# Batches 1 to 7 of an attention and MLP kernel: values read where they lie, key scales by sums, global queries in pairs, and a planner's constants set anew

## The chip, the cores and the metric

The kernel runs on one core of a Trainium2 chip. It is one launch; the metric is the device time of that launch in microseconds (us). The engines that the text speaks of are TensorE (PE; its weight loads are listed as PEld), VectorE (DVE), ScalarE (ACT), GpSimd (POOL) and SyncE (SP), whose queue issues all transfers of this kernel.

## The reference

Attention with a window of 32 and 32 global tokens, over 8 batches and 8 heads, then an MLP with the mish function. Cut to what matters:

```python
k_all, v_all = [k_g, k_l], [v_g, v_l]          # 32 global tokens, 512 local ones, head size 64
out_g = sm(scale * q_g @ k_all.T) @ v_all      # global queries see all 544 keys
s_ll = where(|i - j| <= 32, scale * q_l @ k_l.T, -1e9)
out_l = sm([scale * q_l @ k_g.T, s_ll]) @ [v_g, v_l]
x = [out_g, out_l] as (8 * 544, 512)
h = x @ w_in                                   # 512 x 2048, 64-bit floats
out = (h * tanh(softplus(h))) @ w_out          # 2048 x 512, 64-bit floats
```

## The kernel before

**Attention.** The 8 heads go in pairs (`hp` 0 to 3), so there are 32 pairs (b, hp). Of each pair the 512 local queries are 4 tiles `t` of 128, which gives 128 units (b, hp, t). A tile's scores `s` cover a window of 192 or 224 keys, the global 32 among them (`WIN`). `row_max` masks them and takes the row's maximum on DVE, `expo` is the exponential on ACT, `p_hi` and `p_lo` split the probabilities into two fp16 numbers, `p_turn` transposes them by a DMA (batch 0 does it on PE, `p_pe`), and `pv` multiplies with the values into `U`. A tile's window is taken as two chunks of up to 128 keys. Their values lie in two tiles of their own, `va` and `vc`, which seven DMAs per pair (`v_move`, 416 KB) fill from the split values `vf`. `x_norm` divides, and `x` is transposed into `xx`, from which the MLP reads.

**Global queries.** `g_scores`, `g_max`, `g_exp`, `g_norm` and `g_turn` run once per pair, on 64 rows (2 heads of 32 queries). The stationary operand of `g_scores` is 128 columns wide from batch 2 on, of which the first 64 are used.

**Precision.** fp16 numbers come as a high and a low half, and a product takes three matmuls (hi hi, hi lo, lo hi). The scores of batches 0 and 1 are fp32 matmuls instead (`plain_s`); from batch 2 on `b_norm` takes scales for queries and keys from the largest absolute value of the batch, over 8 loads of 272 KB.

**MLP.** 16 blocks of 256 tokens (two per batch) and one of all global tokens, each in 8 steps: 24 matmuls into `h` (`m1_mm`), mish on ACT into `e` (`mish`), a split into `GG` on DVE (`g_hi`, `g_lo`), 12 matmuls into `o` (`m2_mm`). `h` and `e` have two buffers each, `GG` holds 16 steps. The last three blocks use 7 products in place of 8 (`product`).

**Weights.** They arrive as 64-bit floats in 32 loads of 512 KB (16 for each matrix). Each is turned into fp32 by one ACT instruction and two on DVE (`w_bits`, `w_sum`), enters a norm on PE (`w_stat`), and when the 16 of a matrix are through, `w_norm` sets the scale (one `wd` instruction on DVE begins it) and `w_split` makes the fp16 halves. `h` needs the splits of the first matrix, `o` those of the second.

**Order.** The code does not run in the order in which it is written. `slot(u)` hands tasks with costs to a planner (`Plan`), which works through them by list scheduling and emits each engine's instructions in the order that its plan gives. The first loads stand in `ORDER`, a weight load waits until the planned DMA backlog is under `BULK` ns, and constants such as `CONV1` and `RATE1` give the weights' tasks their places. The planner may also put idle matmuls (`w_s<-consts`) in front of a waiting PE task in the first part. Each engine works its list strictly in order, and the SP queue does too: a DMA that waits for its source holds back all behind it.

Of the kernel before, what the change touches and what calls it, by code (L numbers as in the profile page):

```python
# [1490 lines left out]
```

## Time and profile before

| | |
|---|---|
| median of 3 runs | 925.22 us (923.16 to 926.66) |
| profiled execution: its own time | 922.33 us |
| its span, first to last instruction | 920.5 us |
| PE busy | 894.3 us (97%) |
| DVE, ACT busy | 726.4 us (79%), 612.0 us (66%) |
| mean granted clock of TensorE | 0.988 |
| transfers on the SP queue's ring | 130.65 MB |

Busy PE time is the union of modelled matmul spans. 1.8 us of the profiled execution's time lie outside the span. The profiled execution is 0.8 us under the fastest of the three timed runs and 2.9 us under their median.

### The profile page before, as it was taken

To read this page: it belongs to the slowest core of one execution; us is meant where nothing else is said; L and a number is where in the kernel's file an instruction comes from. 1 tells how busy PE (TensorE), PEld (TensorE's weight loads), DVE (VectorE), ACT (ScalarE), POOL (GpSimd) and SP (SyncE) were. 2 spreads that over 40 slices of the span, in tenths; PEclk is the share of its full clock that TensorE was granted. 3 is DMA by queue.
4 is the path that set the end of the run, shared out by engine and by line. 5 is a ranking of instruction groups with operands and counts; after the bars stand their busy time and mean duration, and the time that the engine had idled before them with its cause. 6 is when DMAs were issued, how large, how long until landed. Compare 5 with 4: busy or idle time off the path is not lost.

```text
span 920.5 us, 21758 instructions
## 1 busy us (share of the span) xinstructions
PE 894.3 (97%) x8444; PEld 649.5 (71%) x8444; DVE 726.4 (79%) x1940; ACT 612.0 (66%) x1309; POOL 18.0 (2%) x30
## 2 busy tenths in 40 slices
PE   4989999999999999999999999999999999999998
PEld 2767866666767766766766766776776776788887
DVE  6999988868878779787987788877876757798761
ACT  5899786877777768776787768776776667322110
POOL 3000000000000000000000000000000000000000
PEclk9799999999999999999999999999999999999999
DMA  9987358987665878667767867777855554100000
GB/s 331 316 260 254 97 138 161 193 185 185 151 147 123 185 162 179 125 154 172 165 128 153 169 158 162 134 184 165 185 114 124 95 88 77 31 13 2 23 13 35
DMA packets 221399, 132.03 MB, mean 143 GB/s; under 512 B 174320, under 2 KB 186736, under 8 KB 221296
## 3 DMA queue, kind: packets, MB, share of 16 engines
q1 hardware_dynamic: 221296, 130.65, 61.6%
q8 instruction: 66, 1.08, 0.5%
q14 instruction: 37, 0.30, 0.1%
HBM read 66.76 MB, written 8.91 MB: 82 GB/s over the span
## 4 chain that ended last, share of the span: by engine, by line
PE 76%; DVE 8%; DMA 7%; ACT 6%; issue 2%; SPq 1%; POOL 0%; ACTq 0%; DVEq 0%
PE h L985 31%; PE o L1050 26%; PE o L1146 5%; PE U L843 4%; PE s L747 3%; PE g L877 2%; DMA pt<-ph 2%; ACT P L771 1%; DMA mx<-in_mxs 1%; PE gu L942 1%; DVE GG L1038 1%; DVE GG L361 1%; SPq L348 1%; DVE P L762 1%; ACT e L1018 1%
## 5 line engine op out<-in xcount | busy, mean ns | idle before, releaser
L985 PE MATMUL h<-xx,W 128*128 128x256 f16 x3072 | 361.6, 273 | 0.3 <-DMA xx<-xs 0.2
L985 PEld LDWEIGHTS <-W 128*128 128x128 f16 x3264 | 311.4, 98 | 43.0 <-issue 4.3
L1050 PE MATMUL o<-W,GG 128*128 128x512 f16 x1344 | 314.5, 379 | 0.9 <-ACT ob L359 0.9
L1050 PEld LDWEIGHTS <-GG 128*128 128x128 f16 x1344 | 128.7, 98 | 128.5 <-issue 2.4
L1018 ACT ACTIVATE e<-h,c 128x512 f32<-128x512 f32 x136 | 92.7, 687 | 125.1 <-PE h L985 108.2
L771 ACT ACTIVATE P<-P,nm 128x192 f32<-128x192 f32 (+1 forms) x256 | 117.6, 461 | 57.8 <-DVE nm L762 56.4
L1038 DVE SCALAR_TENSOR_TENSOR GG<-e,c,GG 128x512 f16<-128x512 f32 (+1 forms) x136 | 111.3, 819 | 3.6
L361 DVE TENSOR_SCALAR GG<-e,c 128x512 f16<-128x512 f32 (+1 forms) x130 | 78.4, 604 | 39.5 <-ACT e L1018 35.1
L762 DVE CUSTOM_DVE_ANT_0 P<-s,consts 128x192 f32<-128x192 f32 (+1 forms) x256 | 87.5, 364 | 4.4 <-PE s L747 4.4
L826 DVE SCALAR_TENSOR_TENSOR ph<-P,ph 128x448 f16<-128x448 f32 (+1 forms) x112 | 62.8, 587 | 23.2 <-ACT ph L359 22.1
L843 PEld LDWEIGHTS <-pt 96*128 96x128 f16 (+1 forms) x1536 | 60.0, 98 | 27.6 <-issue 5.4
L1018 ACT ACT_TABLE_LOAD x55 | 70.6, 1283 | 3.6 <-PE h L985 2.6
L843 PE MATMUL U<-va,pt 128*128 128x64 f16 (+1 forms) x768 | 56.0, 193 | 2.6 <-DMA pt<-ph 2.1
L359 ACT ACTIVATE ph<-P 128x384 f16<-128x384 f32 (+1 forms) x111 | 55.2, 535 | 0.8 <-DMA pt<-ph 0.7
L843 PE MATMUL U<-vc,pt 96*128 96x64 f16 x768 | 55.4, 193 | 0.0
L1146 PEld LDWEIGHTS <-GG 128*128 128x128 f16 x504 | 49.2, 98 | 6.8 <-DVE GG L1038 1.1
L771 ACT ACTIVATION_READ_ACCUMULATOR P<-P,nm 128x1 f32 x256 | 48.1, 188 | 0.0
L359 ACT ACTIVATE ob<-o,c 128x512 f32<-128x512 f32 (+1 forms) x40 | 24.6, 615 | 32.2 <-PE o L1146 26.7
L771 ACT ACT_TABLE_LOAD x34 | 43.6, 1283 | 0.6
L616 DVE TENSOR_REDUCE mx<-mx 128x1 f32<-128x544 f32 x48 | 34.3, 714 | 10.2 <-DMA mx<-in_mxs 10.2
L1146 PE MATMUL o<-W,GG 128*128 128x256 f16 x360 | 41.6, 273 | 0.5 <-DVE GG L1038 0.5
L359 ACT ACTIVATE xg<-gu,sv 64x32 f32<-64x32 f32 x64 | 20.0, 313 | 24.0 <-PE gu L942 23.5
(159 smaller groups left out, 1029.5 us busy)
## 6 DMA issues: line engine op xcount, KB each, us to landing
mx<-in_mxs SPq DMA_DIRECT2D x48, 272.0 KB, 3.1
out<-ob SPq DMA_DIRECT2D x34, 256.0 KB, 2.9
vl<-in_vm SPq DMA_DIRECT2D x32, 256.0 KB, 4.3
W<-in_w SPq DMA_DIRECT2D x15, 512.0 KB, 6.9
...
GG<-in_w SPq DMA_DIRECT2D x11, 512.0 KB, 5.8
```

The costliest lines, as they stand in the source:

```text
L359: A.activation(out=dst, in_=src, func=AF.Copy, scale=c)
L361: V.tensor_scalar(dst, src, c, None, ALU.mult)
L616: pl.add(DVE, dve(544), lambda i=i, k=k: V.tensor_reduce(out=X[mx][:, i:i + 1], in_=X[k][:, :544], axis=AX.X, op=ALU.max, apply_absolute_v ...
L762: pl.add(DVE, 69 + 1.04 * w, lambda: V.tensor_tensor_reduce(out=X[P][:, h, :w], in0=X[s][:, c], in1=mask[:, m0:m0 + w], scale=-SCALE, scal ...
L771: pl.add(ACT, 94 + 0.832 * w + 186, lambda: A.activation(out=X[P][:, h, :w], in_=X[P][:, h, :w], func=AF.Exp, bias=X[nm], scale=-1.0, accu ...
L826: pl.add(DVE, dve(n), lambda: V.scalar_tensor_tensor(p_part(X[ph], t, 1), p_src(X[P], t), PSC, p_part(X[ph], t, 0), ALU.mult, ALU.subtract ...
L843: T.matmul(X[u][:, t, h, :], X[pt][:k, p * 4 + h * 2 + c, :], X[vx][:k, t, vl, h * 64:(h + 1) * 64], start=(n == 0), stop=(n == 5))
L985: T.matmul(X[h][:, f * TB:(f + 1) * TB], wh(i, wl)[:, off:off + 128], X[xx][:, d, x, o:o + TB], start=(n == 0), stop=(n == 11))
L1018: pl.add(ACT, 587, lambda: A.activation(out=X[e][:, 0:4].rearrange("p a n -> p (a n)"), in_=X[h], func=AF.Mish, bias=0.0, scale=X[c][:, 0: ...
L1038: pl.add(DVE, dve(n, 1), lambda: V.scalar_tensor_tensor(gdst(blk, i, 1), gsrc(blk, i), X[c][:, 2:3], gdst(blk, i, 0), ALU.mult, ALU.subtra ...
L1050: T.matmul(X[o], GG[:, r, c + f * 2 + t, g, :], wh(8 + i, wl)[:, f * 512:(f + 1) * 512], start=(i == 0 and n == 0), stop=(i == NF - 1 and ...
L1146: T.matmul(X[o][:, :256], GG[:, r, col, g, :], factor(kind, i, wl), start=(fresh_ and n == 0), stop=(n == 23), skip_group_check=True)
```

## The change

From batch 1 on the keys of a pair are stored as two groups of 128 keys, the 32 global ones and 128 more (576 columns, not 640), so that the own 128 keys of a tile stay one chunk: `pv` reads their values straight from `vf`. Only the edge keys (32 on each side and the global ones) go into a tile `vb`, by four DMAs of 160 KB in all. The probabilities of tiles 1 and 2 are then written in two pieces. Batch 0 keeps the old layout, with `va` in the buffers of `ph`. The scales of queries and keys come from sums of absolute values on ACT, no longer from maxima on DVE. The global queries of two pairs share one tile of 128 rows: each pair's scores are written to its own 64 rows by a stationary operand of 64 columns, and maximum, exponential, norm and transpose run once for two pairs. The last three blocks prefer ACT for `g_hi`. All constants of the planner are others. The core of the diff:

```diff
-KW = 640
+KW, KW0 = 576, 640
...
-WIN = [(0, 192, 32), (128, 224, 0), (288, 224, 0), (448, 192, 0)]
-CHK = [(96, 96), (128, 96), (128, 96), (128, 96)]
-GC = 64
+WIN0 = [(0, 192, 32), (128, 224, 0), (288, 224, 0), (448, 192, 0)]
+CHK0 = [(96, 96), (128, 96), (128, 96), (128, 96)]
+GC0 = 64
+WIN = [(0, 192, 256), (96, 224, 0), (256, 224, 224), (384, 192, 0)]
+EDGE = [64, 128, 96, 128]
+GC = 128
...
-    LOYAL = 844
+    LOYAL = 905
...
-    kept("vc", 2, [96, 4, 2, 128])
-    kept("gph", 1, [64, 2, 640])
-    kept("gP", 1, [64, 640], F32)
+    kept("vb", 2, [128, 4, 2, 128])
+    kept("gph", 1, [128, 2, 640])
+    kept("gP", 1, [128, 640], F32)
...
-            pl.add(DVE, dve(544), lambda i=i, k=k: V.tensor_reduce(
-                out=X[mx][:, i:i + 1], in_=X[k][:, :544], axis=AX.X, op=ALU.max,
-                apply_absolute_value=True), r=[k], w=[[mx, i]] if i else (), new=() if i else [("mx8", mx)])
+            pl.add(ACT, act(544) + 93, lambda i=i, k=k: A.activation(
+                out=X[k][:, :544], in_=X[k][:, :544], func=AF.Abs, accum_out=X[mx][:, i:i + 1]), w=[k] + ([[mx, i]] if i else []),
+                new=() if i else [("mx8", mx)], table="exp")
...
-    def loc(k, j, n):
-
-        a = k[:, 160 * j:160 * j + 64]
-        return bass.AP(a.tensor, a.offset, [list(a.ap[0]), [160, n], [96, 2], list(a.ap[-1])])
+    def loc(k, part, b):
+
+        if b:
+            a, c = k[:, 288 * part:288 * part + 128], [[160, 2]]
+        else:
+            a, c = k[:, 320 * part:320 * part + 64], [[160, 2], [96, 2]]
+        return bass.AP(a.tensor, a.offset, [list(a.ap[0]), *c, list(a.ap[-1])])
...
-        vf, va, vc, g = ("vf", b, hp), ("va", b, hp), ("vc", b, hp), ("vgf", b)
+        vf, vb, g = ("vf", b, hp), ("vb", b, hp), ("vgf", b)
...
-        mv(32, lambda: X[va][0:64, 0], lambda: X[vf][0:64, 0], vf, [va, 0], [("va", va)])
-        mv(128, lambda: X[vc][0:64], lambda: X[vf][64:128], vf, [vc, 0], [("vc", vc)])
-        mv(48, lambda: X[vc][64:96, 0:3], lambda: X[vf][0:32, 1:4], vf, [vc, 1])
-        mv(96, lambda: X[va][32:96, 1:4], lambda: X[vf][0:64, 1:4], vf, [va, 1])
-        mv(48, lambda: X[va][0:32, 1:4], lambda: X[vf][96:128, 0:3], vf, [va, 2])
...
-        mv(48, lambda: X[va][96:128, 1:4], lambda: glob(3), g, [va, 3])
-        mv(16, lambda: X[va][64:96, 0:1], lambda: glob(1), g, [va, 4])
+        if not b:
+            va = ("va", b, hp)
+            mv(32, lambda: first(va)[0:64, 0], lambda: X[vf][0:64, 0], vf, [va, 0], [("ph", va)])
...
+            return
+        if b == 1 and hp < 2:
+            cleared("vb", vb)
+        mv(48, lambda: X[vb][64:96, 1:4], lambda: X[vf][96:128, 0:3], vf, [vb, 0], [("vb", vb)] if vb not in pl.place else [])
+        mv(48, lambda: X[vb][32:64, 0:3], lambda: X[vf][0:32, 1:4], vf, [vb, 1])
+        for n in range(2):
+            mv(32, lambda n=n: X[vb][96 * n:96 * n + 32, n::2], lambda: glob(2), g, [vb, 2 + n])
+
...
+    def cleared(tag, x):
+
+        pl.add(POOL, 1100, lambda: G.memset(X[x], 0.0), new=[(tag, x)])
...
+    PIECES = [((0, 0, 192),), ((0, 64, 192), (192, 32, 32)), ((32, 0, 192), (0, 192, 32)), ((0, 64, 192),)]
+
+    def pieces(t, P, ph, part):
+
+        return [(X[P][:, :, a:a + n], X[ph][:, part, :, c:c + n], X[ph][:, 0, :, c:c + n]) for a, c, n in PIECES[t]]
...
     def p_hi(b, hp, t):
-        P, ph, n = ("P", b, hp, t), ("ph", b, hp, t), 2 * WIN[t][1]
-        pl.add([(ACT, act(n)), (DVE, dve2(n))], 0, lambda e: scaled(e, p_part(X[ph], t, 0), p_src(X[P], t), PSC), r=[P], new=[("ph", ph)])
+        P, ph = ("P", b, hp, t), ("ph", b, hp, t)
+
+        def go(e):
+            for x, y, _ in pieces(t, P, ph, 0):
+                scaled(e, y, x, PSC)
+        zero = (b, hp) == (1, 0) and t < 2
...
-        P, ph, n = ("P", b, hp, t), ("ph", b, hp, t), 2 * WIN[t][1]
-        pl.add(DVE, dve(n), lambda: V.scalar_tensor_tensor(p_part(X[ph], t, 1), p_src(X[P], t), PSC, p_part(X[ph], t, 0),
-                                                           ALU.mult, ALU.subtract), r=[P], w=[ph])
+        P, ph = ("P", b, hp, t), ("ph", b, hp, t)
+
+        def go():
+            for x, y, hi in pieces(t, P, ph, 1):
+                V.scalar_tensor_tensor(y, x, PSC, hi, ALU.mult, ALU.subtract)
+        pl.add(DVE, pcost(t, dve), go, r=[P], w=[ph])
...
-                for c, vx in ((0, va), (1, vc)):
-                    k = CHK[t][c]
+                if b:
+                    chunks = (t % 2, X[vf], 128), (1 - t % 2, X[vb], EDGE[t])
+                else:
+                    chunks = (0, first(va), CHK0[t][0]), (1, X[vb], CHK0[t][1])
+                for c, vx, k in chunks:
                     for p, vl in ((0, 0), (0, 1), (1, 0)):
-                        T.matmul(X[u][:, t, h, :], X[pt][:k, p * 4 + h * 2 + c, :], X[vx][:k, t, vl, h * 64:(h + 1) * 64],
+                        T.matmul(X[u][:, t, h, :], X[pt][:k, p * 4 + h * 2 + c, :], vx[:k, t, vl, h * 64:(h + 1) * 64],
...
-        def products(out, terms):
-            a = 0 if part else 32
-            for c0, n, rhs in ((a, 256, lambda k: loc(k, 2 * part, 2)), (0, 32, lambda k: k[:, GC:GC + 32]))[:2 - part]:
-                for i, (x, k) in enumerate(terms):
-                    T.matmul(X[g][:out, c0:c0 + n], x, rhs(k), start=(i == 0), stop=(i == len(terms) - 1))
-
...
-        two = lambda n: X[q][:, n, hp:hp + 2, :].rearrange("p a q -> p (a q)")
-        pl.add(PE, mm(3, 262) + (1 - part) * 80, lambda: products(128, [(two(0), X[ks]), (two(1), X[ks]), (two(0), X[kl])]),
-               r=[ks, kl, q], new=bank(g))
+        g = ("g", b, hp, part)
+        a, gc = 0 if part else 32, GC if b else GC0
+        for n in range(2):
+            rows = slice(64 * n, 64 * n + 64)
...
+            def products(terms, rows=rows):
+                for c0, w, rhs in ((a, 256, lambda k: loc(k, part, b)), (0, 32, lambda k: k[:, gc:gc + 32]))[:2 - part]:
+                    for i, (x, k) in enumerate(terms):
+                        T.matmul(X[g][rows, c0:c0 + w], x, rhs(k), start=(i == 0), stop=(i == len(terms) - 1))
+
+            where = dict(w=[g]) if n else dict(new=bank(g))
...
+            pl.add(PE, mm(3, 262) + (1 - part) * 80, lambda n=n, ks=ks, kl=kl, q=q, products=products: products(
+                [(X[q][:, 0, hp + n], X[ks]), (X[q][:, 1, hp + n], X[ks]), (X[q][:, 0, hp + n], X[kl])]), r=[ks, kl, q], **where)
...
-            P, s, d, T_ = ("gP", b, hp), ("gs", b, hp), ("gd", b, hp), ("gT", b, hp)
...
-            pl.add(from_ps(320), 0, lambda e: copy(e, flat(0), X[T_][:, :320]), r=[T_], new=[("gpt", pt)])
...
+        P, s, d = ("gP", b, hp), ("gs", b, hp), ("gd", b, hp)
+        pl.add(DVE, dve2(128, 1), lambda: V.tensor_scalar(X[d], ident, X[s][:, 3:4], None, ALU.mult), r=[s, "consts"], new=[("gd", d)])
+        for c0, n in ((0, 3), (3, 2)):
...
+            pl.add(PE, mm(1, w + 5), lambda T_=T_, w=w, flat=flat: T.matmul(X[T_][:, :w], nid, flat(0), start=False, stop=True, skip_group_check=True),
...
-        pl.add([(DVE, dve2(n, 1)), (ACT, act(n, 1))], 0, lambda en: scaled(en, gdst(blk, i, 0), gsrc(blk, i), X[c][:, 2:3]), r=[e, [c, 2]],
+        pl.add([(DVE, dve2(n, 1)), (ACT, act(n, 1))][::1 if blk < FAST else -1], 0, lambda en: scaled(en, gdst(blk, i, 0), gsrc(blk, i), X[c][:, 2:3]), r=[e, [c, 2]],
...
-        if t == 2:
+        if t == 2 and hp % 2 == 0:
...
-    BULK = 5486.64
-    LAG = 13
-    ORDER = "m q0 w10 w1 q2 k0 w3 b w0 w5 k1 q1 g k3 w8 w11 k2 w2 q3 w14 w4 w12 w9 w6 w7 w13 w15"
-    CONV1 = 0.898
-    RATE1 = 0.011
-    CONV2 = 0.591
...
+    BULK = 2300.851
+    LAG = 9
+    ORDER = "k0 b w10 q0 w0 w5 w4 w8 w14 w1 q3 g m w3 q2 k1 k3 w11 k2 w12 w2 w7 w6 w13 w9 q1 w15"
+    CONV1 = 2.527
+    RATE1 = 0.155
+    CONV2 = 0.02
...
-    lb = k_l.reshape(B, H, 16, 32, D)
-    gb = k_g.reshape(B, H, 1, 32, D)
-    blocks = [x for t in range(4) for x in (lb[:, :, 4 * t:4 * t + 2], gb, lb[:, :, 4 * t + 2:4 * t + 4])]
...
+    lb = k_l.reshape(B, H, 4, 128, D)
+    blocks = [lb[:, :, 0], k_g, lb[:, :, 1], lb[:, :, 2], k_g, lb[:, :, 3]]
     kt = once(np.concatenate(blocks, axis=2).reshape(B, HP, 2, KW, D))
```

How the order moves, at three places. First the SP queue at the program's start (`W` and `wraw` are weight loads of 512 KB, `kn`, `qn`, `vl` keys, queries and values of batch 0). Before:

```order
L348 DMA consts_65<-in_consts 128x352
L348 DMA qn_0_0_103<-in_qt 128x512
L348 DMA W_74<-in_w1 128x2x512
L348 DMA wraw_0_106<-in_w1 128x2x512
L348 DMA qn_0_1_108<-in_qt 128x512
L348 DMA kn_0_0_111<-in_kt 128x640
L348 DMA wraw_2_114<-in_w1 128x2x512
```

After, from the queue's 16th transfer on; ahead of it stand only keys, queries, values and constants (`ph0_86<-vf`, `vb0_90<-vf` are `v_move` of pair 0):

```order
L352 DMA masks_66<-in_masks 128x448
L352 DMA vgraw_1_160<-in_vg 128x128
L352 DMA ph0_86<-vf_0_0_155 64x256
L352 DMA vb0_90<-vf_0_0_155 64x1024
L352 DMA vb0_90<-vf_0_0_155 32x768
L352 DMA ph0_86<-vf_0_0_155 64x768
L352 DMA ph0_86<-vf_0_0_155 32x768
L352 DMA ph0_86<-vgf_0_152 32x3x256
L352 DMA ph0_86<-vgf_0_152 32x256
L352 DMA W_75<-in_w1 128x2x512
L352 DMA ph1_87<-vf_0_1_162 64x256
```

The first weight load moves from the queue's 3rd place to its 25th, behind the seven moves of pair 0, which wait for that pair's split values.

Second, VectorE's first rows of work on weights (L457 and L471 before, L461 and L475 after). Before, right behind the constants:

```order
L1424 TENSOR_SCALAR nid_68<-consts_65 128x128
L457 SCALAR_TENSOR_TENSOR W_74<-W_74 128x512
L471 SCALAR_TENSOR_TENSOR W_74<-W_74 128x512
L457 SCALAR_TENSOR_TENSOR W_74<-wraw_0_106,W_74 128x512
L471 SCALAR_TENSOR_TENSOR W_74<-wraw_0_106,W_74 128x512
L762 ISA P0_77,nm_0_0_0_0_144<-s_0_0_0_0_134,consts_65 128x192
```

After, behind the row maxima of all four tiles of pair 0 (`P3` is the fourth tile's) and the values' maxima:

```order
L789 ISA P3_81,nm_0_0_3_1_216<-s_0_0_1_1_175,consts_65 128x192
L789 ISA nm_0_0_3_1_216 128x1
L828 SCALAR_TENSOR_TENSOR pt_0_0_1_224<-T_0_0_1_209,pt_0_0_1_224 128x512
L891 TENSOR_SCALAR rs_0_0_235<-sums_0_0_167 128x8
L892 RECIPROCAL rs_0_0_235<-rs_0_0_235 128x8
L934 TENSOR_REDUCE gmx_0_0_254<-g_0_0_0_221 128x1
L461 SCALAR_TENSOR_TENSOR W_75<-W_75 128x512
L475 SCALAR_TENSOR_TENSOR W_75<-W_75 128x512
```

The conversions stand in front of the attention of pair 0 before, and behind most of it after.

Third, TensorE ahead of the first `o` product (`h_1_0` is step 0 of block 1). Before:

```order
L985 MATMUL h_0_6_1590<-xx_0_509,W_74 128x256
...
L985 MATMUL h_0_7_1629<-xx_0_509,W_74 128x256
L985 LDWEIGHTS W_74
...
L985 MATMUL h_1_0_1677<-xx_0_509,W_74 128x256
...
L1050 LDWEIGHTS GG_76
L1050 MATMUL o_0_0_1719<-W_74,GG_76 128x512
```

After:

```order
L1030 MATMUL h_1_0_1631<-xx_0_447,W_75 128x256
...
L1030 MATMUL h_1_1_1660<-xx_0_447,W_75 128x256
...
L1030 MATMUL h_1_2_1696<-xx_0_447,W_75 128x256
L1030 LDWEIGHTS W_75
...
L1030 MATMUL h_1_3_1748<-xx_0_447,W_75 128x256
...
L1095 LDWEIGHTS GG_77
L1095 MATMUL o_0_0_1786<-W_75,GG_77 128x512
```

Nine steps of `h` (block 0 and one of block 1) stand ahead of the first `o` before, twelve after.

## Rows read from the trace of the kernel before

**Rows 1.** Busy time by engine in four stretches of the span:

```profile
core 0: us, PE busy (x) PEld busy (x) DVE busy (x) ACT busy (x) POOL busy (x), PEclk, DMA share, GB/s
0.00:88.00 88.00, 70.20 (x670) 53.01 (x671) 76.21 (x219) 70.45 (x175) 8.94 (x16) 0.88 0.90 296
88.00:119.00 31.00, 30.20 (x266) 24.69 (x264) 29.46 (x81) 25.18 (x51) 0.71 (x2) 1.00 0.44 102
119.00:900.00 781.00, 777.56 (x7368) 557.62 (x7365) 618.22 (x1638) 514.43 (x1081) 8.31 (x12) 1.00 0.61 131
900.00:921.00 21.00, 16.38 (x149) 14.20 (x146) 2.51 (x5) 1.89 (x4) 0.00 (x0) 0.95 0.07 26
```

**Rows 2.** Timeline of TensorE in the steady part, start and length:

```profile
420.03 2.79 PE L985 MATMUL h<-xx,W 128*128 128x256 f16 x24
422.65 2.75 PE L1050 MATMUL o<-W,GG 128*128 128x512 f16 x12
...
431.72 0.25 PE L843 MATMUL U<-va,pt 128*128 128x64 f16 x3
431.81 0.25 PE L843 MATMUL U<-vc,pt 96*128 96x64 f16 x3
431.99 0.26 PE L747 MATMUL s<-ks,qs 64*128 64x192 f16 x2
...
432.35 0.26 PE L747 MATMUL s<-kl,qs 64*128 64x224 f16 x2
432.44 0.26 PE L747 MATMUL s<-ks,qs 64*128 64x224 f16 x2
432.64 0.61 PE L985 MATMUL h<-xx,W 128*128 128x256 f16 x4
```

**Rows 3.** Timeline of TensorE: first products, first h, first o:

```profile
9.70 1.75 PE L747 MATMUL s<-kn,qn 64*128 64x192 f32 x8 [9.70 <-DMA kn<-in_kt]
...
89.76 0.65 PE L877 MATMUL g<-kn,qgraw 128*64 128x256 f32 x2
...
90.68 1.47 PE L985 MATMUL h<-xx,W 128*128 128x256 f16 x12
...
112.66 6.71 PE L985 MATMUL h<-xx,W 128*128 128x256 f16 x60
119.20 5.13 PE L1050 MATMUL o<-W,GG 128*128 128x512 f16 x23
```

**Rows 4.** Timeline of VectorE: first conversion, x of batch 0 done, second norm:

```profile
6.71 0.69 DVE L457 SCALAR_TENSOR_TENSOR W<-W 128x512 int32<-128x512 int32 x1 [3.05 <-ACT W L456]
...
86.53 0.68 DVE L853 TENSOR_TENSOR x<-U,rs 128x512 f32<-128x512 f32 x1
...
113.44 0.28 DVE L500 CUSTOM_DVE_ANT_0 wd<-w_s,consts 128x128 f32<-128x128 f32 x1
```

**Rows 5.** Groups of VectorE by line and form:

```profile
L616 DVE TENSOR_REDUCE mx<-mx 128x1 f32<-128x544 f32 x48 | 34.3, 714 | 10.2 <-DMA mx<-in_mxs 10.2
...
L891 DVE TENSOR_REDUCE gmx<-g 64x1 f32<-64x288 f32 x32 | 14.3, 446 | 6.1 <-PE g L877 5.9
...
L471 DVE SCALAR_TENSOR_TENSOR W<-W 128x512 int32<-128x512 int32 x15 | 10.3, 687 | 0.3
```

**Rows 6.** Groups of ScalarE:

```profile
L1018 ACT ACT_TABLE_LOAD x55 | 70.6, 1283 | 3.6 <-PE h L985 2.6
...
L771 ACT ACTIVATION_READ_ACCUMULATOR P<-P,nm 128x1 f32 x256 | 48.1, 188 | 0.0
...
L899 ACT ACTIVATE gP<-g,gmx 64x288 f32<-64x288 f32 x32 | 15.8, 494 | 5.0 <-DVE gmx L894 4.6
```

**Rows 7.** Timeline of the SP queue, each row the issue of transfers:

```profile
1.65 0.43 SPq L348 DMA_DIRECT2D W<-in_w  x1
...
19.74 0.57 SPq L348 DMA_DIRECT2D va<-vf  x1
...
21.03 1.13 SPq L348 DMA_DIRECT2D vc<-vf  x2
```

**Rows 8.** DMA issues by line: KB each, median us to landing:

```profile
W<-in_w SPq DMA_DIRECT2D x15, 512.0 KB, 6.9
...
vc<-vf SPq DMA_DIRECT2D x32, 128.0 KB, 2.7
```

**Rows 9.** Groups of weight loads of the global scores:

```profile
L877 PEld LDWEIGHTS <-qgh 128*128 128x128 f16 x216 | 15.9, 97 | 1.7
...
L877 PEld LDWEIGHTS g<-kn,qgraw 128*64 128x64 f32 x48 | 5.0, 136 | 4.7 <-DVE sv L369 1.1 <-DVE nm L762 0.7 <-ACT xg L359 0.5
```

More of the change, by code (lines that the diff above doesn't have):

```diff
@@ L557, in plain_load @@
         name, part = pair(b, hp, kind)
-        pl.add(DMA, dma(n / 2), lambda: load(X[name][:, part], src[b * HP + hp]), w=[[name, part]],
+        pl.add(DMA, dma(n / 2), lambda: load(X[name][:, part, :n], src[b * HP + hp]), w=[[name, part]],
                new=() if name in pl.place else [(kind, name)])
@@ L566, in b_load @@
         if what == "g":
-            pl.add(DMA, dma(160), lambda: load(X["qgraw", b], qg[b]), new=[("qgraw", ("qgraw", b))])
+            pl.add(DMA, dma(128), lambda: load(X["qgraw", b], qg[b]), new=[("qgraw", ("qgraw", b))])
             return
@@ L899, in g_exp @@
             pl.add(ACT, 464, lambda part=part, c0=c0, c1=c1: A.activation(
[L900 removed]
+                out=X[P][:, 96 + c0:96 + c1], in_=X["g", b, hp, part][:, 0:c1 - c0], func=AF.Exp, bias=X[mx][:, 2:3], scale=SCALE,
                 accum_out=X[s][:, part:part + 1]), r=[mx, ("g", b, hp, part)], w=[[P, part], [s, part]],
@@ L932, in g_turn, with turned @@
-        turn(160, lambda: X[pt], lambda: X[ph].rearrange("p a k -> p (a k)"), r=[ph], new=[("gpt", pt)])
+        if not by_pe(b):
+            turn(320, lambda: X[pt], lambda: X[ph].rearrange("p a k -> p (a k)"), r=[ph], new=[("gpt", pt)])
+            return
+        P, s, d = ("gP", b, hp), ("gs", b, hp), ("gd", b, hp)
+        pl.add(DVE, dve2(128, 1), lambda: V.tensor_scalar(X[d], ident, X[s][:, 3:4], None, ALU.mult), r=[s, "consts"], new=[("gd", d)])
+        for c0, n in ((0, 3), (3, 2)):
+            T_, w = ("gT", b, hp, c0), n * 128
+            def turned(T_=T_, c0=c0, n=n):
+                for c in range(n):
+                    T.matmul(X[T_][:, c * 128:c * 128 + 128], X[P][:, (c0 + c) * 128:(c0 + c) * 128 + 128], X[d], start=(c == 0), stop=(c == n - 1))
+            pl.add(PE, n * 426 + 100, turned, r=[P, d], new=[("h", T_)], rows=0.3)
+            flat = lambda part, c0=c0, n=n: X[pt][:, part * 5 + c0:part * 5 + c0 + n].rearrange("p a q -> p (a q)")
+            pl.add(from_ps(w), 0, lambda e, T_=T_, w=w, flat=flat: copy(e, flat(0), X[T_][:, :w]), r=[T_], w=[[pt, c0]], new=() if c0 else [("gpt", pt)])
+            pl.add(PE, mm(1, w + 5), lambda T_=T_, w=w, flat=flat: T.matmul(X[T_][:, :w], nid, flat(0), start=False, stop=True, skip_group_check=True),
+                   r=[[pt, c0], "ids"], w=[T_])
+            pl.add(from_ps(w), 0, lambda e, T_=T_, w=w, flat=flat: copy(e, flat(1), X[T_][:, :w]), r=[T_], w=[[pt, c0]])
@@ L939, in go @@
             for c in range(5):
-                vv = X[vf][:, c - 1] if c else X[va][:, 1]
+                vv = X[vf][:, c - 1] if c else X[vx][:, 1] if b else first(vx)[:, 1]
                 for p, vl in ((0, 0), (0, 1), (1, 0)):
-                    T.matmul(X[u][:, :64], vv[:, vl, :], X[pt][:, p * 5 + c, :], start=(n == 0), stop=(n == 14))
+                    T.matmul(X[u][:, :64], vv[:, vl, :], X[pt][:, p * 5 + c, half:half + 64], start=(n == 0), stop=(n == 14))
                     n += 1
-        pl.add(PE, mm(15, 69), go, r=[pt, vf, va], new=bank(u))
+        pl.add(PE, mm(15, 69), go, r=[pt, vf, vx], new=bank(u))
         for h in range(2):
@@ L1287, in slot @@
             att(x_turn, *vu)
-        if t == 2:
+        if t == 2 and hp % 2 == 0:
             att(g_exp, b, hp)
@@ L1324, in slot @@
             v_move(0, hp1)
+        if u == 8:
+            pl.add(DMA, dma(224), lambda: load(masks, masks_in), w=["masks"])
         if u in (8, 15):
```

149 lines of the change are left out of this document (77 added, 72 removed).

## The prediction

> **What bounds the kernel now.** I read the busy time by stretches first. The rows cut the span at 88, 119 and 900 us [rows 1]. From 119 to 900 us TensorE works 777.56 of 781.00 us: 3.4 us idle, so in this stretch only TensorE's own work counts. In the last 21 us it idles 4.6 us, for the last product and the output. From 88 to 119 us it idles 0.8 us. From 0 to 88 us it idles 17.8 us, and part of its 70.20 busy us there are idle matmuls that the planner puts in front of waiting tasks, so in this stretch TensorE waits for others: VectorE is busy 76.21 us, ScalarE 70.45 us.
>
> The timeline of TensorE then gives two marks [rows 3]: the first `h` at 90.68 us and the first `o` at 119.20 us. From the first `h` on there is always some `h` to fill with, up to the limit that the order sets. The first `o` needs the second matrix's scale and splits; the instruction that begins that scale on VectorE, `wd`, runs at 113.44 us [rows 4]. So the end is
>
> end = time of the first `o` + TensorE's work that the order puts behind it + idle time behind it.
>
> The steady rate is in the timeline: 24 matmuls of `h` from 420.03 to 422.65 us, 109.2 ns each [rows 2].
>
> The profiled execution took 922.33 us, its span is 920.5 us, so 1.8 us lie outside. It is 2.9 us under the median of 925.22 us. I make the sum against 922.3 and carry the difference over to the median.
>
> **1. What stands ahead of the first `o`.** By the order, nine steps of `h` stand ahead of it before and twelve after: 216 and 288 matmuls. 72 x 109.2 ns [rows 2] = 7.9 us of work leave the stretch behind the first `o`. One more pair of fp32 global scores does so too: two visits such as the one at 89.76 us, 0.65 us each [rows 3], 1.2 us with their overlap. Together **-9.1 us**, if they really find time ahead of the first `o`. For that the first `h` has to come earlier. It stands behind the `x` of batch 0's last pair, on VectorE at 86.53 us [rows 4]. I added up VectorE's instructions ahead of that place in both orders, each with the mean of its row: 74.2 us before, 62.2 after, because 57 weight instructions of 0.69 us (such as those of L471 [rows 5]) stand ahead of it before and 41 after. So I expect that `x` some 8 to 10 us earlier, after allowing 2 to 4 us for the later start (next part), and the first `h` at 80 to 82 us. From 81 to 121 us are 40 us; 288 x 0.1092 = 31.4 us of `h`, and some 5 us of attention as before (28.5 us from first `h` to first `o`, less 216 x 0.1092 = 23.6), fit with 3 to 4 us to spare.
>
> **2. When the first `o` comes.** VectorE's work ahead of `wd`, added up in the same way, is 100.2 us before and 98.4 after: three maxima of `b_norm` less, at 714 ns [rows 5], fewer reductions of global queries at 446 ns [rows 5] since they run for two pairs, and three more splits of `GG` on it. VectorE's idle time up to 119 us is 119 - 76.21 - 29.46 = 13.3 us [rows 1]. After, the weights are late: the first weight load was issued at 1.65 us [rows 7] and takes 6.9 us [rows 8], so VectorE converts from 6.71 us [rows 4]. After, it is behind pair 0's seven moves, which wait for that pair's split values; before, the first of them left at 19.74 us, some 0.57 us of issue each [rows 7]. I take the first conversion at about 21 us, since pair 0 is no longer held up by weight loads in front of its keys (first score at 9.70 us, on a key load [rows 3]). VectorE then has only attention to do up to there, and idles 3 to 5 us more. 98.4 - 100.2 + 3 to 5 = **+1.5 us** (1.2 to 3.2): the first `o` at about 121 us. Lower bound 0, if pair 0's attention fills the hole; upper bound +10, if SP's queue passes its wait on (below).
>
> **3. Global queries in pairs.** From batch 2 on, 24 visits of 9 matmuls become 12 of 18; each now has a stationary operand of 64 columns and writes 64 of PSUM's 128 rows. No row shows that shape in fp16. For the load: 97 ns with 128 columns in fp16, 136 ns with 64 columns in fp32 [rows 9]; 39 ns x 216 = 8.4 us is the upper bound, were loads never hidden. The matmuls themselves stream as many columns as before. For entering and leaving another shape, the nearest row is the scores' 64-row stationary operand: from `U` at 431.81 us to `s` at 431.99 us, 0.18 where neighbours are 0.09 apart, and from 432.44 to `h` at 432.64, 0.20 for 0.09 [rows 2]: 0.2 us per visit, 12 x 0.2 = 2.4 us. The upper bound is 8.4 + 2.4 = 10.8 us, the lower 0 (a gain is excluded, as the columns stay the same). I take **+2 us**, as the loads' form is nearest to the hidden fp16 one.
>
> The Trainium skill speaks against this edit: "TensorEngine Tiling (Array Packing)", under Key Properties, says that a change of the tiling mode drains TensorE, and under Restrictions that column tiling disables the fast weight load. The gaps of 0.09 and 0.11 us agree with the first, for row tiling. No run here shows the second; by it the upper bound, and not +2, would stand in the sum.
>
> **4. The stretch from 119 to 900 us.** Most of the change lies here, beside TensorE's work. VectorE loses 45 maxima (32 us at 714 ns [rows 5]), half of the global reductions and 26 splits of `GG` that go to ScalarE. By the order it falls from 726 us to about 650. ScalarE takes the absolute sums: 48 x about 0.55 us plus the read of the accumulator, 188 ns [rows 6], +36 us; second pieces of `p_hi` (+0.2 us for 56 tiles), +11; the splits of `GG`, +16; the global exponentials of 494 ns [rows 6] are halved, as is what goes with them, -21. That is some +40 on 514.43 us in this stretch, 71% busy where it was 66% [rows 1]: still covered by TensorE. Table loads (1283 ns [rows 6]) stay nearly the same in number, since the absolute value is planned within exp's set; were each sum to bring its own, +61 us, ScalarE would still be at 79%. An absolute sum has no row: it lies between a bare ScalarE instruction of its width and the same with its accumulator, and twice it would add 36 us, also under the cover. The second pieces of `p_lo` (0.1 to 0.3 us each on VectorE) and the four clearings on POOL, which is busy 8.31 of 781 us [rows 1], cost nothing for the same reason; without cover each second would stand in full, 11 and 4 us. Transfers shrink by 256 KB a pair and three issues of 0.57 us [rows 7]; moves landed in 2.7 us [rows 8], two units ahead of their use, with the DMA engines 61% busy [rows 1]: hidden either way. What is left to gain is the 3.4 us of idle time [rows 1], part of it a wait for such transfers: I take **-1.5 us** (-3.4 to 0).
>
> **5. Tail.** The last `o` and its output follow as before: 0, the 4.6 us idle stay [rows 1]. Splitting `GG` on ScalarE in the last blocks trades two engines that are 2.51 and 1.89 us busy in 21 [rows 1]; a late split would show as a wait of `o`.
>
> **Sum:** 922.3 - 9.1 + 1.5 + 2 - 1.5 = 915.2, 7.1 us less; on the median 925.2 - 7.1 = **918 us**.
>
> **The rivals.** *A: the gain is given back (no change).* `h` may run ahead only as fast as ScalarE and VectorE empty it: it has two buffers, and each step needs a mish and a split. VectorE is busy 29.46 of 31 us and ScalarE 25.18 from 88 to 119 us [rows 1], while they still convert the second matrix. Three more steps there cost them some 2 us each, and the second scale comes that much later: first `o` at +5 to +7, sum -9.1 + 6 + 2 - 0.5 = -1.6: about 924. Against it: the sums of part 2 hold these steps already. Chance 0.20.
>
> *B: the queue passes its wait on (slower).* The weights stand behind moves that wait for split values, and SP's queue is strictly in order. If pair 0's values are split at 30 us rather than 19.74 [rows 7], the first conversion comes 10 us later, and 32 weights must follow in a stretch whose DMA share is 0.90 already [rows 1]. First `o` at +12 or more: -9.1 + 12 + 2 = +5: about 930. It decides from a first conversion at about 28 us. For it: the DMA share, and ScalarE, which splits those values, is 80% busy. Against it: with the weights away, pair 0's values come at once. Chance 0.12.
>
> *C: the 64-column operand pays in full (slower).* +10.8 in place of +2: 926 to 927, and up to 929 if entry costs more than the scores' 0.2. This is what the page's rule would do here. Chance 0.08.
>
> *D: more gain.* Part 3 costs nothing, first `o` stays at 119 us, all idle time of part 4 goes: -9.1 + 0 + 0 - 3.4 = -12.5: 912 to 913. Chance 0.15.
>
> **Numbers.** The forecast has 0.45. Its own range is 914 to 921. About 0.5% (4.6 us) is what a measurement of this kernel can tell from no change: below 920.6 is faster, above 929.8 slower. Faster: D and nearly all of the forecast, 0.56. Slower: part of B and the edge of C, with a late stall anywhere, 0.13. The rest, 0.31, is the same. The range of 909 to 926 holds D's bound with some us for stalls gone that I don't see, the forecast and A, and leaves out B and most of C.
>
> **What would show it.** First `h` at 80 to 82 us and first `o` at 119 to 122, with twelve steps of `h` between: part 1 and 2 right. First conversion at 20 to 22 us: B wrong; at 28 or later: B right. `h` of steps 10 to 12 with waits for `e` ahead of them: A. Gaps of more than 0.2 us round the visits of `g`, or loads of its operand above 97 ns that stand bare: C. TensorE idle over 4 us from the first `o` to 900 us: part 4 wrong. The prediction fails most easily at the first `o`, since each us there moves the end by one, and it rests on VectorE's order, which I added up without its waits.

## The result: slower, and the profile after

The changed kernel takes 933.83 us (median of 6 runs, 933.04 to 935.41), the kernel before 922.95 us in the same comparison; the ratio is 1.0116 (1.0099 to 1.0132). The forecast was 918 us. The profiled execution took 933.04 us, its span is 931.2 us: 10.7 us more than the 920.5 us of before.

The busy time by stretches, with the columns of [rows 1]:

```profile
0.00:88.00 88.00, 64.36 (x641) 48.39 (x642) 65.92 (x202) 62.35 (x159) 11.77 (x20) 0.90 0.84 267
119.00:900.00 781.00, 777.23 (x7284) 550.06 (x7284) 535.33 (x1536) 548.46 (x1181) 7.35 (x14) 1.00 0.55 120
```

TensorE idles 23.6 us up to 88 us (17.8 before) and 3.8 us from 119 to 900 us (3.4 before). The long stretch is as full as it was, and VectorE and ScalarE have changed in it nearly as forecast (535 us, 83 less, and 548 us, 34 more). So the 10.7 us lie in two places: ahead of the first `h`, where TensorE waits, and in TensorE's own work, if that has grown. The timeline of TensorE shows the two marks of [rows 3]:

```profile
89.78 5.40 PE L1030 MATMUL h<-xx,W 128*128 128x256 f16 x48
...
129.88 2.75 PE L1095 MATMUL o<-W,GG 128*128 128x512 f16 x12
...
426.77 0.26 PE L883 MATMUL U<-vf,pt 128*128 128x64 f16 x3
426.96 0.26 PE L883 MATMUL U<-vb,pt 64*128 64x64 f16 x3
427.15 0.26 PE L883 MATMUL U<-vf,pt 128*128 128x64 f16 x3
427.34 0.26 PE L883 MATMUL U<-vb,pt 64*128 64x64 f16 x3
427.53 2.79 PE L1030 MATMUL h<-xx,W 128*128 128x256 f16 x24
432.75 0.25 PE L883 MATMUL U<-vf,pt 128*128 128x64 f16 x3
432.84 0.25 PE L883 MATMUL U<-vb,pt 128*128 128x64 f16 x3
...
433.10 2.79 PE L1030 MATMUL h<-xx,W 128*128 128x256 f16 x24
...
457.70 1.47 PE L1030 MATMUL h<-xx,W 128*128 128x256 f16 x12
459.10 0.41 PE L920 MATMUL g<-ks,qgh 128*64 128x256 f16 x2
459.35 0.27 PE L920 MATMUL g<-kl,qgh 128*64 128x256 f16 x1
459.45 0.21 PE L920 MATMUL g<-ks,qgh 128*64 128x32 f16 x2
...
459.52 0.41 PE L920 MATMUL g<-ks,qgh 128*64 128x256 f16 x4
459.76 0.28 PE L920 MATMUL g<-kl,qgh 128*64 128x256 f16 x2
459.87 0.21 PE L920 MATMUL g<-ks,qgh 128*64 128x32 f16 x2
...
460.19 0.27 PE L920 MATMUL g<-kl,qgh 128*64 128x256 f16 x1
460.39 0.83 PE L1030 MATMUL h<-xx,W 128*128 128x256 f16 x6
```

The first `h` comes at 89.78 us, hardly earlier than before, and the first `o` at 129.88 us, 10.7 us later. Behind the first `o` both spans have 801.3 us left, although 72 matmuls of `h` fewer stand there now.

What took their place is in the rows of `U`. For tile 0 the edge chunk has 64 rows (`EDGE = [64, ...]`; the form is 64\*128), the own chunk 128. The four groups start 0.19 us apart, and the visit takes 427.53 - 426.77 = 0.76 us. For a tile with 128 rows in both chunks they start 0.09 us apart, and the visit takes 0.35 us. The start-to-start times of all `U` rows, with waits left out, sum to 59.1 us, against 48.8 us before: +10.3 us.

The rows of `g` show the other shape that the prediction had priced: 18 matmuls of the 64-column operand in 460.39 - 459.10 = 1.29 us. Summed like `U`, the fp16 global scores take 15.45 us, against 17.54 before: -2.1 us. But entering the shape costs time too, and that falls into the row ahead: from the last matmul of `h` to the first of `g` it is 0.20 us where 0.11 is usual, in 12 visits 1.1 us. Leaving it costs as much (460.39 - 460.19 = 0.20) and is in the sum. So the net is -1.0 us. What pays for the two changes is in the middle of the visit: six matmuls of 256 columns take 0.35 us (459.52 to 459.87), no more than the first three (459.10 to 459.45). Before, each such matmul started 0.11 us behind the last one.

The start on VectorE, which [rows 4] showed for the kernel before (first conversion, `x` of batch 0's last pair, `wd` of the second matrix):

```profile
18.09 0.41 DVE L934 TENSOR_REDUCE gmx<-g 128x1 f32<-128x288 f32 x1
22.35 0.69 DVE L461 SCALAR_TENSOR_TENSOR W<-W 128x512 int32<-128x512 int32 x1 [3.85 <-ACT W L460]
23.69 0.42 DVE L934 TENSOR_REDUCE gmx<-g 128x1 f32<-128x256 f32 x1
...
85.94 0.69 DVE L893 TENSOR_TENSOR x<-U,rs 128x512 f32<-128x512 f32 x1
...
124.84 0.29 DVE L504 CUSTOM_DVE_ANT_0 wd<-w_s,consts 128x128 f32<-128x128 f32 x1 [0.71 <-PE w_s L497]
```

and its busy time up to that `x`, with what it waited for up to 88 us (releaser, us in total, times, longest; the last line is the kernel before):

```profile
0.00:85.94 85.94, 62.34 (x631) 47.53 (x632) 63.86 (x194) 60.30 (x153) 10.24 (x19) 0.90 0.83 268
```

```profile
DVE W L461 <- ACT W L460: 8.6, 5, 3.9
DVE vmx L591 <- DMA vl<-in_vm: 5.2, 2, 4.4
DVE vmx L591 <- DMA vm<-in_vm: 1.7, 1, 1.7
...
DVE W L457 <- ACT W L456: 4.3, 3, 3.1
```

VectorE has 63.9 us of work ahead of that `x` (74.7 before, up to 86.53 us), as added up from the order, but 22.1 us of idle time in place of 11.8. It waits 8.6 us for weights, 4.3 us more than before, and 6.9 us for loads of values (`vl`, `vm`), for which it did not wait before. Of these 6.9 us, 4.4 are its first wait in the program; before, it waited 2.3 us there for the constants. The late first weight stands in VectorE's order between the two halves of a global maximum (18.09 and 23.69 us), so attention waits for it too.

### The profile page after: what moved, and what is told of

The parts are those of the page before. It is cut to its first block, busy times and chain, and to the rows that moved or that the text cites. A ratio compares the mean times of both kernels' runs of the same rounds, so it can differ in the third digit from the quotient of the medians.

```text
span 931.2 us, 21570 instructions
## 1 busy us (share of the span) xinstructions
PE 899.0 (97%) x8442; PEld 647.2 (69%) x8442; DVE 639.4 (69%) x1813; ACT 645.6 (69%) x1402; POOL 19.1 (2%) x34
## 4 chain that ended last, share of the span: by engine, by line
PE 81%; DVE 7%; DMA 6%; ACT 2%; SPq 2%; issue 1%; POOL 0%; ACTq 0%
PE h L1030 35%; PE o L1095 28%; PE o L1191 6%; PE U L883 5%; PE s L773 4%; DMA pt<-ph 2%; SPq L352 2%; PE g L920 2%; PE gu L987 1%; DMA W<-in_w 1%; DMA gpt<-gph 1%; DVE W L461 1%; DVE W L475 1%; DVE P L789 1%; DVE W L534 1%
## 5 line engine op out<-in xcount | busy, mean ns | idle before, releaser
L365 DVE TENSOR_SCALAR GG<-e,c 128x512 f16<-128x512 f32 x104 | 50.2, 483 | 75.8 <-ACT e L1063 75.7
L789 DVE CUSTOM_DVE_ANT_0 P<-s,masks 128x192 f32<-128x192 f32 (+1 forms) x224 | 75.9, 368 | 19.8 <-PE s L773 19.7
L883 PEld LDWEIGHTS <-pt 128*128 128x128 f16 (+2 forms) x1536 | 64.4, 98 | 35.1 <-issue 10.8
L863 DVE SCALAR_TENSOR_TENSOR ph<-P,ph 128x384 f16<-128x384 f32 x168 | 67.2, 442 | 23.5 <-ACT ph L363 22.8
L363 ACT ACTIVATE ph<-P 128x384 f16<-128x384 f32 (+1 forms) x164 | 60.5, 419 | 2.1 <-DMA pt<-ph 1.4
L883 PE MATMUL U<-vb,pt 128*128 128x64 f16 (+2 forms) x768 | 57.8, 193 | 0.0
L883 PE MATMUL U<-vf,pt 128*128 128x64 f16 x672 | 50.5, 194 | 2.2 <-DMA pt<-ph 2.2
L363 ACT ACTIVATE GG<-e,c 128x896 f16<-128x896 f32 (+1 forms) x32 | 30.7, 959 | 20.6 <-PE o L1191 11.2
L620 ACT ACTIVATE mx<-mx 128x544 f32<-128x544 f32 x48 | 31.4, 654 | 9.6 <-DMA mx<-in_mxs 8.1
L363 ACT ACTIVATE xg<-gu,sv 64x32 f32<-64x32 f32 x60 | 18.8, 314 | 22.5 <-PE gu L987 22.1
```

The source lines that it names most:

```text
L363: A.activation(out=dst, in_=src, func=AF.Copy, scale=c)
L365: V.tensor_scalar(dst, src, c, None, ALU.mult)
L789: pl.add(DVE, 69 + 1.04 * w, lambda: V.tensor_tensor_reduce(out=X[P][:, h, :w], in0=X[s][:, c], in1=mask[:, m0:m0 + w], scale=-SCALE, scal ...
L863: V.scalar_tensor_tensor(y, x, PSC, hi, ALU.mult, ALU.subtract)
L883: T.matmul(X[u][:, t, h, :], X[pt][:k, p * 4 + h * 2 + c, :], vx[:k, t, vl, h * 64:(h + 1) * 64], start=(n == 0), stop=(n == 5))
```

## Experiments on the shape of `U`

Theory S: each change between a 128-row and a 64-row stationary operand costs TensorE about 0.1 us. Rival L: these gaps are not real, the loss is that of the late first `o` alone.

**edge96**: one number of the changed kernel.

```diff
-EDGE = [64, 128, 96, 128]
+EDGE = [96, 128, 96, 128]
```

> One number of the changed kernel: the edge chunk of tile 0 is multiplied with 96 rows in place of 64 (the 32 rows more hold zeros); the order of every engine stays the same. Theory S (TensorE waits about 0.1 us at each change between a 128-row and a 64-row stationary operand, four changes per pair, 28 pairs): the visits of U for tile 0 shrink from 0.76 to 0.36 us, time behind the first o falls by 28 x 0.4 = 11 us at most, by 10 as U's own gain in the two traces is: 933.8 - 10 = 924 (922.5 to 925). Rival L (the loss is the late first o alone, the gaps in U are hidden or only modelled): 933 to 934, first o at 130 us either way.

Measured: 924.55 us against 923.65 of before, ratio 1.0011 (0.9997 to 1.0026): 9.3 us less than the changed kernel. The first `o` stays at 130.2 us. TensorE's timeline:

```profile
422.63 0.26 PE L883 MATMUL U<-vf,pt 128*128 128x64 f16 x3
422.73 0.25 PE L883 MATMUL U<-vb,pt 96*128 96x64 f16 x3
...
423.00 2.78 PE L1030 MATMUL h<-xx,W 128*128 128x256 f16 x24
```

The visit takes 0.37 us, 0.39 less. 28 of them make 10.9 us, and the `U` rows sum to 48.3 us (waits left out). Rows of 96 and of 128 mix without a gap. S holds, L falls.

**half_changes**: the second head of tile 0 takes its edge chunk first.

```diff
-                for c, vx, k in chunks:
+                for c, vx, k in chunks[::-1] if b and t == 0 and h else chunks:
```

> The changed kernel with its 64-row edge chunk, but for tile 0 the second head takes its two chunks in reverse order (edge chunk first), so that a visit has two changes between 128 and 64 rows in place of four; same products, same order of everything else. Theory S (the price is per change): half of the 9 to 10 us comes back: 933.8 - 5 = 929 (928 to 930), the visit 0.56 us in place of 0.76. Rival P (the price is that of 64-row products, or one per visit): 933 to 934.

Measured: 928.62 us, 5.2 us under the changed kernel, ratio to before 1.0055 (1.0032 to 1.0077). The timeline has two gaps in place of four:

```profile
423.84 0.26 PE L883 MATMUL U<-vf,pt 128*128 128x64 f16 x3
424.04 0.35 PE L883 MATMUL U<-vb,pt 64*128 64x64 f16 x6
424.31 0.26 PE L883 MATMUL U<-vf,pt 128*128 128x64 f16 x3
424.41 2.79 PE L1030 MATMUL h<-xx,W 128*128 128x256 f16 x24
```

0.20 us from `vf` to `vb` for three matmuls, 0.27 for six of them, 0.10 to `h`: the visit takes 0.57 us. Half the changes, half the price (`U` sums to 53.8 us): it is paid per change, not by the 64-row products.

**b_rows64**: the same shape put into the kernel before.

```diff
-                    k = CHK[t][c]
+                    k = 64 if (t, c) == (0, 0) else CHK[t][c]
```

> The kernel before with 64 rows in place of 96 in the first chunk of tile 0; the products with the last 32 rows of that chunk (the global keys of tile 0) are left out. Theory S: the same four changes per pair come into the kernel before: 28 pairs x 0.4 = 11 us, batch 0 mostly beside other waits: 922.95 + 11 = 934 (932 to 935). Rival L: 923, or less, since no product is shorter and none is longer.

Measured: 928.63 us, ratio 1.0056 (1.0041 to 1.0072): 5.0 us more, half of what S said. The timeline tells why:

```profile
422.57 0.24 PE L747 MATMUL s<-ks,qs 64*128 64x192 f16 x2
422.65 0.25 PE L843 MATMUL U<-va,pt 64*128 64x64 f16 x3
422.83 0.26 PE L843 MATMUL U<-vc,pt 96*128 96x64 f16 x3
423.03 0.26 PE L843 MATMUL U<-va,pt 64*128 64x64 f16 x3
423.22 0.26 PE L843 MATMUL U<-vc,pt 96*128 96x64 f16 x3
423.31 2.79 PE L985 MATMUL h<-xx,W 128*128 128x256 f16 x24
```

In this order the visit often follows scores `s`, which have 64 rows themselves: the change from `s` to `U` falls away (0.08 us, no gap). `U` sums to 58.4 us (+9.6), `s` to 28.9 (-2.1), and TensorE's idle time falls by 1.3 us (26.2 to 24.9). The expectation had counted four changes and forgot the neighbour: 25 of the 32 visits follow `s`, and such a visit has three changes and takes one away from `s`. The price per change stands: 32 visits of three changes at 0.10 us are the 9.6 us.

## Experiments on the start

With 96 rows the kernel is as fast as before (ratio 1.0011); the gain of the forecast is still missing. Its first `h` is 8 us later than forecast. Theory W: the weights come late because their loads stand behind other transfers in the SP queue. Rival N: the new code itself makes the start late.

**edge96_early** and **edge96_oldconst**: edge96 with ORDER and BULK of the kernel before, and with all its constants.

```diff
-    BULK = 2300.851
+    BULK = 5486.64
...
-    ORDER = "k0 b w10 q0 w0 w5 w4 w8 w14 w1 q3 g m w3 q2 k1 k3 w11 k2 w12 w2 w7 w6 w13 w9 q1 w15"
+    ORDER = "m q0 w10 w1 q2 k0 w3 b w0 w5 k1 q1 g k3 w8 w11 k2 w2 q3 w14 w4 w12 w9 w6 w7 w13 w15"
```

> The kernel with the 96-row edge chunk, and of the planner's constants ORDER and BULK as before: the first weight loads stand at places 4, 5 and 8 of the SP queue again, not 25, 33 and 36, and 8 steps of h stand ahead of the first o. Theory W (the late weight loads leave VectorE, and TensorE ahead of the first h, idle): TensorE's idle time up to 90 us falls from 18 to 24 back to 12, first conversion at 7 to 8 us, first o before 122 us, time 6 us under the 96-row kernel: 917 to 919. Rival N (the new code itself, not the place of the loads, makes the start late): within 2 us of the 96-row kernel, 922 to 926.

> The kernel with the 96-row edge chunk and all of the planner's constants as before; 6 steps of h stand ahead of the first o. Theory W: TensorE's idle time ahead of the first h as before the change, the savings of the new code (global queries in pairs, 2 us on TensorE in the steady part and 4 us of transposes at the start) stay: 916 to 920. Rival N: 922 to 926. If the steady part needed the new constants, TensorE's idle time from 130 to 900 us is over 6 us and the time over 925.

Measured: 921.65 us (ratio 0.9983, 0.9968 to 0.9997) and 923.38 us (0.9998, 0.9983 to 1.0012). In edge96_early the first `h` comes at 84.97 us, 4.6 us earlier. Busy time of its engines, up to the `x` at 81.30 us and from 12 to 40 us:

```profile
0.00:81.30 81.30, 61.36 (x611) 46.79 (x612) 68.21 (x205) 64.64 (x160) 10.69 (x19) 0.87 0.92 302
12.00:40.00 28.00, 21.37 (x171) 15.52 (x169) 25.88 (x71) 22.02 (x56) 0.71 (x1) 0.76 1.06 349
```

VectorE idles 13.1 us up to that `x` and works 25.9 us from 12 to 40 us. But TensorE still idles 19.9 us up to 88 us, where W expected 12, only 8 steps of `h` stand ahead of the first `o`, and the time falls by 2.9 us, not 6. 921.65 us lies between W's range and N's, 923.38 us in N's. edge96_oldconst has its first `h` 3.5 us earlier than edge96 and its first `o` 13.5 us earlier, but with 6 steps ahead of that `o` and not 12, 144 matmuls (15.7 us) more stand behind it.

**b_newconst**: the kernel before with all the new constants.

> The kernel before with all the planner's constants of the changed one; first weight loads at places 17, 26 and 35 of the SP queue, 9 steps of h ahead of the first o as before. Theory W (late weight loads starve VectorE at the start): VectorE's busy time from 12 to 40 us falls from 26 us to 17 to 20, TensorE's idle and filler time ahead of the first h grows by 3 to 8 us: 923.6 + 3 to 8 = 927 to 932. Rival N (the start is late by the new code): 922 to 925.

Measured: 948.52 us, ratio 1.0271 (1.0243 to 1.0299), worse than either theory said.

```profile
0.00:95.47 95.47, 72.44 (x706) 54.77 (x706) 71.30 (x215) 68.41 (x171) 8.43 (x16) 0.91 0.80 264
12.00:40.00 28.00, 21.10 (x170) 15.25 (x169) 17.40 (x58) 20.03 (x55) 0.00 (x0) 0.76 0.79 262
```

VectorE idles 24.2 us up to that `x` (11.8 with the old constants) and works 17.4 us from 12 to 40 us, as W said; the first `h` comes at 99.5 us. The rest of the loss, 17 us in the profiled execution, lies behind the first `o`, where TensorE under the new constants idles 10.7 us more from 130 to 880 us.

**edge96_bulk** and **edge96_bulk4000**: edge96 with BULK alone at 5486.64, and at 4000.

> The kernel with the 96-row edge chunk and one constant as before, BULK (a weight load waits until the planned backlog is under it): first weight loads at places 8, 10 and 11 of the SP queue, 5 steps of h ahead of the first o. Theory W: VectorE's busy time from 12 to 40 us above 22 us (17.0 with the late loads), first h at or before 85 us, 920 to 922. Rival N: 924 to 926.

> The kernel with the 96-row edge chunk and BULK at 4000 in place of 2300.9: first weight loads at places 8, 10 and 33 of the SP queue, 8.5 steps of h ahead of the first o. Theory C (the order of the engines' work decides, not the place of the first loads alone): no forecast from the place of the loads, 919 to 932 by how the order falls out; the first h and the steps of h ahead of the first o give the time together: first h at 85 us with 8 steps as in the kernel with ORDER and BULK as before would be 921 to 922. Theory W (the place of the first loads alone): 920 to 922.

Measured: 933.09 us (1.0112, 1.0084 to 1.0140) and 933.43 us (1.0121, 1.0103 to 1.0139). The first conversion came at 10.6 and 11.3 us, as early as W wants it, and yet the first `h` at 91.1 and 98.2 us. Both times lie outside every range that was given. That the place of the first loads alone decides is refuted.

**edge96_poolq**: edge96, the first matrix's loads on GpSimd's queue; the compute engines' rows are in the same order.

```diff
-                load(dst.rearrange("p (c f) -> p c f", c=2),
+                G.dma_start(dst.rearrange("p (c f) -> p c f", c=2),
```

> The kernel with the 96-row edge chunk; the first matrix's weight loads of 512 KB (those of the first 8 column blocks) are issued on GpSimd's queue, so that they no longer stand behind the v_moves on the SP queue; the order of TensorE, VectorE and ScalarE is the same in every row. Theory W: the first weight lands before 16 us, not at 21.5, VectorE's first conversion comes 5 us or more earlier, its busy time from 12 to 40 us rises from 17 to over 20 us, the first h comes at or before 87 us and the time falls by 2.5 to 5 us: 919.5 to 922. Rival D (the transfers share the DMA engines, what VectorE waits for is the sum of the bytes and not the queue): first h at 89 to 91 us, 924 to 926.

Measured: 926.74 us, ratio 1.0035 (1.0017 to 1.0053): no faster than edge96. The first loads were issued at 9.71, 10.59 and 11.31 us, not from 17.71 us on, and VectorE converted at 18.51 us, not 23.15. The first `h` came at 90.95 us, in D's range. What VectorE waited for:

```profile
DVE gmx L934 <- PE g L920: 5.9, 1, 5.9
...
DVE W L461 <- ACT W L460: 2.3, 3, 1.6
```

TensorE's row ahead of that `g`, and ScalarE's rows behind it:

```profile
22.19 0.32 PE L883 MATMUL U<-ph,pt 96*128 96x64 f16 x3 [5.10 <-DMA ph<-vgf]
```

```profile
26.66 0.50 ACT L942 ACTIVATE gP<-g,gmx 128x288 f32<-128x288 f32 x1 [8.19 <-DVE gmx L937]
...
28.08 0.76 ACT L460 ACTIVATE W<-wraw,two 128x512 f32<-128x512 uint16 x1
```

The wait for weights fell (8.5 us in edge96, 2.3 here), and another took its place. Pair 0's last move `ph<-vgf` now runs beside three loads of 512 KB and lands late (from 8 to 30 us such moves of 48 KB took 6.0 us to land, 2.1 in edge96), `U` waits 5.1 us for it, the second half of `g` stands behind `U`, the maximum behind `g`, the exponential behind the maximum. The second weight, issued at 10.59 us, stands behind that exponential in ScalarE's order and is converted at 28.08 us. Neither side of the expectation had this: the bytes compete, as D said, but the order of the engines passes the wait on.

**edge96_lessmove**: the moves of batch 0 cut to a quarter (in the five `mv` calls from `vf`, `[0:64]` becomes `[0:16]`, and so on).

> The kernel with the 96-row edge chunk, in which batch 0's moves of own and edge values carry a quarter of their rows (88 in place of 352 KB a pair; the rest of these values stays zero and so is left out); same number of transfers, same order on every engine. Theory D (the start waits for the sum of the bytes): 1.06 MB less at some 310 GB/s is 3.4 us of the transfers ahead of the first h, first h at 86 to 88 us, 921.5 to 923. Rival C (it waits for the chain of engines in the order: conversion, maximum, exponential, transpose, each behind the other): first h within 1 us of 89.6, 924 to 925.5.

Measured: 925.17 us, ratio 1.0022 (1.0009 to 1.0035), first `h` at 91.0 us. 264 KB a pair less gain nothing. That the bytes of these moves decide is refuted. C's time came; its first `h` missed by 0.4 us (within 1 us of 89.6). The chain that it names is what is left, and no run shows it by itself.

Six kernels together. VectorE's columns go to `x` of batch 0's last pair (busy from the windows, idle the rest):

| kernel | us | first `h` | first `o` | steps ahead | VectorE busy | idle |
|---|---|---|---|---|---|---|
| before | 923.7 | 90.7 | 119.2 | 9 | 74.7 | 11.8 |
| b_newconst | 948.5 | 99.5 | 130.7 | 9 | 71.3 | 24.2 |
| edge96_oldconst | 923.4 | 86.1 | 116.7 | 6 | 69.5 | 12.2 |
| edge96 | 924.6 | 89.6 | 130.2 | 12 | 63.8 | 22.0 |
| edge96_early | 921.7 | 85.0 | 116.1 | 8 | 68.2 | 13.1 |
| edge96_bulk | 933.1 | 91.1 | 119.0 | 5 | 70.2 | 17.1 |

Lines 1 to 4 are two codes under two sets of constants. The new code brings the first `h` earlier, by 4.6 us under the old constants and by 9.9 under the new. The new constants bring it later, by 8.8 us in the old code and 3.5 in the new, all through VectorE's idle time. So N falls. W holds for the constants as a set; it falls for the queue place of the first loads alone.

## Why the prediction was wrong

**Steps that held.** The relation of the end to the first `o` held: 129.88 + 801.3. The moved work is there: from edge96, behind the first `o` 921.6 - 130.2 = 791.4 us are left, 9.9 us less than before, where the terms -9.1, +2 and -1.5 made -8.6. That these are so near is partly luck: `g` came to -1.0 us and not +2, and the idle time behind the first `o` grew by 0.9 us where it was to fall by 1.5. VectorE's work ahead of batch 0's last `x` was added up as 74.2 and 62.2 us; the windows show 74.7 and 63.9. The first conversion was put at about 21 us and came at 22.35. The long stretch hid ScalarE's new work: an absolute sum took 654 ns on ScalarE and its accumulator's read 187, where 550 and 188 were forecast, and from 130 to 900 us TensorE's waits are for transposes by DMA alone.

**The step that failed first: the price of the row count was put on `g` and not on `U`.** Part 3 read 0.09 and 0.11 us for entering and leaving a 64-row operand from the scores [rows 2], and charged them to the global scores. The diff gives `pv` a 64-row operand too (`EDGE`), between two of 128 rows, four changes a visit, 28 visits. 28 x 0.39 = 10.9 us, from rows that were already in hand, was left out of the sum. edge96 and half_changes show it.

The rule of the Trainium skill ("TensorEngine Tiling (Array Packing)", Key Properties) that a change of mode drains TensorE was the right one, and the trace agrees: 0.09 to 0.11 us per change, for rows and for columns. It was held against one edit, `g`, and not against the other.

**The step that failed second: VectorE's idle time at the start was taken as 2 to 4 us more (3 to 5 up to the first `o`).** It was 10.3 us more. So the first `h` came at 89.8, not 81 us. From there to the first `o` TensorE was full for 40.1 us (0.7 us of gaps), as long as forecast, and the first `o` came at 129.9, not 121. VectorE's side tells the same: up to `wd` it works 100.6 us and idles 24.2, before 100.9 and 12.6. I had added up each engine's work and given the late weights one hole, at the beginning. Shown in its place: the new set of constants makes VectorE idle 22 us, in many waits, of which those for weights (8.6 us, 4.3 before) and for values (6.9, none before) are the largest; under the old constants the same code idles 12.2 us. Not shown is which constant does it: the runs that removed a single wait got another one (edge96_poolq) or the same (edge96_lessmove), and those that changed BULK alone got a different order altogether.

**A term that was too high:** the global queries in pairs. +2 us was forecast, and a gain was excluded "as the columns stay the same"; it is -1.0. The two changes of shape cost 0.19 us per visit, as read from [rows 2]. But six of a visit's matmuls start in pairs, 5 ns apart in place of 109, which the prediction did not expect. Products of two pairs write different halves of the tile's rows; that this lets them run side by side is likely and not shown by a run of its own. Loads of 64 columns take 110 ns, more than the 97 of 128 columns [rows 9], but are hidden behind matmuls of 256 columns.

```profile
L920 PEld LDWEIGHTS <-qgh 128*64 128x64 f16 x216 | 13.0, 110 | 2.7 <-issue 2.7
```

The Trainium skill ("TensorEngine Tiling (Array Packing)", Restrictions) says that column tiling disables the fast weight load. The trace is in line with it, since half the columns take longer (110 ns). The 10.8 us that rival C counted did not come.

**The sum again**, against the profiled execution: 915.2 forecast, 933.0 measured. +9.2 for the first `o` (10.7 for 1.5), +9.8 for `U` (behind the first `o` 51.3 us for 41.5: 10.9 for the changes, less 1.1 in its other rows), -3.0 for `g` (-1.0 for +2), +1.9 for the 1.5 us of idle time that were to go and did not (3.4 became 3.8): +17.9, of 17.8 to account for.

**The rivals.** B named a late first `o` by weights behind moves, but put its point at a first conversion of 28 us; 10.7 us were lost at 22.35. A's pacing of `h` was not seen: the largest wait of `h` for `e` ahead of the first `o` is 0.32 us. C's size came, by another edit, which is chance.

**A version at least as fast as both:** edge96_early, 921.65 us, 12.2 us under the changed kernel. Its 0.17% under the kernel before (0.9968 to 0.9997) is less than what I call a difference here.
